# The order of P5 and P6 by halves of d_ff, and of one layer-2 unit, in a sparse attention and MLP kernel

## The chip, the cores and the metric

One core of one Trainium2 chip. The core has five engines with an instruction queue each, which run beside each other and wait for each other by semaphores: TensorE (PE in the profile; its weight loads are shown as PEld), VectorE (DVE), ScalarE (ACT), GpSimd (POOL) and SyncE (SP, which here only issues DMAs). The metric is the device time of the whole kernel in microseconds (us). Before the change it is 301.54 us, the median of three runs (301.05 to 302.14).

## The reference

Sparse attention over 8 batches, 8 heads, 576 positions and head size 64, in two patterns, and then a two-layer MLP with a leaky activation over the 4608 tokens:

```python
rel = pos[:, None] - pos[None, :]
mask_local = (rel >= 0) & (rel < stride)                  # stride 32; heads 0 to 3
mask_strided = (rel >= 0) & (pos[None, :] % stride == pos[:, None] % stride)   # heads 4 to 7
scores = np.where(masks[None], scale * np.matmul(q, k.transpose(0, 1, 3, 2)), -1000000000.0)
attn = np.exp(scores - scores.max(-1, keepdims=True))
attn_out = np.matmul(attn / (attn.sum(-1, keepdims=True) + 1e-09), v)
x = attn_out.transpose(0, 2, 1, 3).reshape(4608, 512)
h = x @ w_in                                              # w_in 512 x 2048
g = np.maximum(h, 0.0) + alpha * np.minimum(h, 0.0)
out = g @ w_out                                           # w_out 2048 x 512
```

## The kernel before

Everything that is multiplied is float16, sums are float32 in PSUM. The tokens are worked through in nine chunks of 512 (`n` = 0 to 8). A chunk has a layer 1 and a layer 2; between these matmuls stand the pieces of the attention whose output the next chunks need. One program order is written out by hand: each helper records its instructions with `keep`, and on every engine they stand in the order in which they were recorded.

Layer 1 (`lin1_piece`, L573): for each of the 16 blocks of d_ff, four matmuls into a PSUM tile `hps`, a negative part on ScalarE (`neg`, L593) and a combination on VectorE into `gT` (L596, recorded one step later).

Layer 2 of chunks 2 to 8 (`lin2_fast`, L673) uses seven products of half size in place of eight, P1 to P7, on sums of blocks. Each of them has, for each of two blocks of 128 tokens (`r`; in the products by sums a token half `z`), eight matmuls of 128x256 over the eight pairs of d_ff blocks (`y`). The sums of `wout` are made once (`wsum`, four tiles), those of `gT` once a chunk (`gsum`, four tiles, L643 and L654): each is made in two halves, `h` = 0 for y 0 to 3 and `h` = 1 for y 4 to 7, on VectorE or GpSimd. The table `sums` says behind which of the chunk's 30 steps; steps 0 to 15 are layer 1, 16 and 17 are P1, 18 and 19 P5, 20 and 21 P6, then P2, P7, P3, P4 (P4 and P3 are interleaved in the last chunk):

```python
sums = {
    5: [(2, 0, "pool")], 9: [(0, 0, "pool")], 15: [(0, 1, "dve"), (1, 0, "dve")],
    16: [(1, 1, "dve")], 18: [(2, 1, "dve")], 19: [(3, 0, "dve")], 20: [(3, 1, "dve")]}
```

P5 is gsum0 by wsum0, P6 is gsum1 by wsum1. In chunks 2 to 7 P5 already takes its halves of d_ff one after the other, for both token halves each (`both`, matmuls at L709); P6 takes one token half with all eight `y`, and then the other (L719). In the last chunk P5 does so too, and its second token half goes to a PSUM tile of its own, `bank["f"]`. P1 goes to bank a and is copied to bank b (L733), on which P6 and then P7 and P4 add; P5 stands in bank e. ScalarE copies P5 and P6 to `par` tiles in SBUF (L736, in the last chunk L727 for each half of P5), which VectorE adds to later results on their way out (`store`, L656, L665).

Attention pieces run between these steps (`attn_step`, L557): scores of a pair of heads (`score_both`, L333, matmuls at L353, into one `sp` tile of two banks and two `sph` tiles), the exp on ScalarE (L376, L382), the mask on GpSimd (L378, L385), the product with v (`pv_piece`, L390, matmuls L406), and its scaling on VectorE (reciprocal L413, multiply L415, into `x16` or `x16s`). `pv`, `sph`, transposed tiles `tp` and `xp` all come from one pool of three PSUM buffers (`pspool`), used in turn: each waits until the engine that reads the buffer's last content has read it.

Layer 2 of chunk 0 is spread by hand over the attention of batch 1 (list at L901). `U(kf)` is a unit of three 128x512 matmuls (L875) for one block of d_ff, into three PSUM tiles that no attention piece uses; `W(i)` does the chunk's last 128 tokens. `T(2, "q")` and `T(2, "k")` turn the local heads' q and k (`transpose_piece`, L254, nine transposes at L269 into two `tp` tiles, copied to SBUF by ScalarE, L207, and VectorE, L209). `Pv(g, i)` is the i-th product with v of pair g. The stretch that the change touches runs `Pv(7, 1), U(6), T(2, "q"), Pv(7, 2), U(7), T(2, "k"), Pv(6, 1), U(8)`.

Of the kernel before, what the change touches and what calls it, by code (L numbers as in the profile page):

```python
# [9 lines left out]
F32 = mybir.dt.float32  # L10
# [22 lines left out]
def kernel(  # L33
# [10 lines left out]
    nc = tc.nc  # L44
    keep = tc.keep_in_program_order
# [15 lines left out]
    npool = ctx.enter_context(tc.tile_pool(name="np", bufs=2))  # L61
    opool = ctx.enter_context(tc.tile_pool(name="op", bufs=4))
    pspool = ctx.enter_context(tc.tile_pool(name="ps", bufs=3, space=bass.MemoryType.PSUM))
# [8 lines left out]
    wsum = [cpool.tile([128, 8, 256], F16, name=f"wsum{i}") for i in range(4)]  # L72
    gsum = [cpool.tile([128, 8, 256], F16, name=f"gsum{i}") for i in range(4)]
# [180 lines left out]
    def transpose_piece(u, nm):  # L254

        b = u // 2  # L260
        early = b < NEARLY
        src = cast16[(b, False, nm)]
        dst = qTs[u % 2][:, :, 0:576] if nm == "q" else kTs[u % 2][:, :, 32:608]
        o = dst.rearrange("r e (p t) -> r e p t", t=9)
        tps = []
        for t0, t1 in ((0, 5), (5, 9)):
            tp = pspool.tile([128, 8, 64, 2], F16, tag="ps", name="tp")
            for t in range(t0, t1):
                keep(nc.tensor.transpose(  # L269
                    tp[:, t - t0].rearrange("r p e -> r (p e)"), src[:, t].rearrange("p f d -> p (f d)"), ident))  # L270
            tps.append(tp[:, 0 : t1 - t0].rearrange("r t p e -> r e p t"))
        cast_copy("act", o[:, :, :, 0:5], tps[0])
        cast_copy("dve" if early and (u or nm == "k") else "act", o[:, :, :, 5:9], tps[1])
# [116 lines left out]
    def pv_piece(P, a):  # L390
        while defer and any(P.et[z][0] is defer_et["et"] for z in P.et):
            defer.pop(0)()
        if P.x16 is None:
            if P.xd and P.strided:
                P.x16 = x16s
            else:
                P.x16 = xpool.tile([128, 1024], F16, tag="x16", name="x16")
        v16 = cast16[(P.b, P.strided, "v")]
        grp = P.pgroups[a]
        r = 72 if P.strided else 128  # L400
        pv = pspool.tile([128, 512], F32, tag="ps", name="pv")
        nb = 2 * len(grp)
        for x in range(nb):
            t, hh = grp[x // 2], x % 2
            et, c = P.et[(t, hh)]
            keep(nc.tensor.matmul(  # L406
                pv[:, 65 * x : 65 * x + 65], et[0:r, c : c + 128],
                v16[0:r, 2 * P.pr + hh, t, :] if P.strided else v16[:, 6 * (2 * P.pr + hh) + t, :],
                start=(x == 0), stop=(x == nb - 1), skip_group_check=True))
        w = P.w  # L410
        rc = rpool.tile([128, 8], F32, tag="rc", name="rc")
        pvv = pv[0:w, 0 : 65 * nb].rearrange("r (c e) -> r c e", e=65)
        keep(nc.vector.reciprocal(rc[0:w, 0:nb], pvv[:, :, 64]))  # L413
        c0 = 128 * grp[0]
        keep(nc.vector.tensor_tensor(  # L415
            P.x16[0:w, c0 : c0 + 64 * nb].rearrange("r (c e) -> r c e", e=64),
            pvv[:, :, 0:64],
            rc[0:w, 0:nb].unsqueeze(2).to_broadcast([w, nb, 64]), op=ALU.mult))
# [46 lines left out]
    def T(u, nm):  # L465
        return lambda: transpose_piece(u, nm)
# [4 lines left out]
    def Pv(g, i):  # L471
        return lambda: pv_piece(pairs[g], i)
# [198 lines left out]
    bank = {}  # L671

    def lin2_fast(n, i):  # L673

        last = n == NCH - 1
        x, r = (("1", i) if i < 2 else ("5", i - 2) if i < 4 else ("6", i - 4) if i < 6 else ("2", i - 6) if i < 8
                else ("7", i - 8) if i < 10 else ("3", i - 10) if i < 12 else ("4", i - 12))  # L680
        if last and i > 10:
            x, r = (("4", 0), ("4", 1), ("3", 1))[i - 11]
        b = {"1": "a", "2": "a", "5": "e", "3": "e"}.get(x, "b")
        first = x in "15" and r == 0
        if first:
            bank[b] = phpool.tile([128, 512], F32, tag="hps", name="ops")
        o = bank[b][:, 256 * r : 256 * r + 256]
        if last and b == "e" and r == 1:
            if x == "5":
                bank["f"] = pspool.tile([128, 512], F32, tag="ps", name="opsl")  # L690
                first = True
            o = bank["f"][:, 0:256]

        def g(t, j):
            return lambda y: gTs[n][:, 2 * y + j, 256 * t + 128 * r : 256 * t + 128 * r + 128]

        def s(z):
            return lambda y: gsum[z][:, y, 128 * r : 128 * r + 128]

        def w(j, c):  # L700
            return lambda y: wout16[:, 2 * y + j, 256 * c : 256 * c + 256]

        def t(z):
            return lambda y: wsum[z][:, y, :]

        def both(h):
            for z in range(2):
                for y in range(4 * h, 4 * h + 4):
                    keep(nc.tensor.matmul(  # L709
                        bank["e"][:, 256 * z : 256 * z + 256], gsum[0][:, y, 128 * z : 128 * z + 128], wsum[0][:, y, :],  # L710
                        start=(z == 0 and y == 0), stop=(y == 7), skip_group_check=True))

        lhs, rhs = {
            "1": (g(0, 0), w(0, 0)), "2": (g(0, 1), w(1, 0)), "3": (s(3), w(1, 1)),
            "4": (g(1, 1), t(3)), "5": (s(0), t(0)), "6": (s(1), t(1)), "7": (s(2), t(2))}[x]
        if x == "5" and not last:
            both(r)
        for y in range(8 if x != "5" or last else 0):
            keep(nc.tensor.matmul(  # L719
                o, lhs(y), rhs(y), start=(first and y == 0), stop=(y == 7), skip_group_check=True))  # L720
        if last and x == "3":
            store(n, 0, 1, bank["f" if r else "e"], bank["s6"], r)
            return
        if last and x == "5":
            if r == 0:
                bank["s5"] = npool.tile([128, 512], F32, tag="par", bufs=2, name="par")
            keep(nc.scalar.copy(bank["s5"][:, 256 * r : 256 * r + 256], o))  # L727
            return
        if r == 0:
            return  # L730
        if x == "1":
            bank["b"] = phpool.tile([128, 512], F32, tag="hps", name="ops")
            keep(nc.scalar.copy(bank["b"], bank["a"]))  # L733
        elif x in "56":
            z = npool.tile([128, 512], F32, tag="par", bufs=2, name="par")
            keep(nc.scalar.copy(z, bank[b]))  # L736
            bank["s" + x] = z
        elif x == "2":
            store(n, 0, 0, bank["a"])
        elif x == "7":  # L740
            late.append(lambda: store(n, 1, 1, bank["b"], bank["s5"]))
        elif x == "3":
            late.append(lambda: store(n, 0, 1, bank["e"], bank["s6"]))
        else:
            store(n, 1, 0, bank["b"])
# [12 lines left out]
    def warm(n):  # L758

        for _ in range(n):  # L760
# [12 lines left out]
            name=nc.get_next_instruction_name(), act_func_set_id=6, ins=[], outs=[]  # L773
# [96 lines left out]
    def U(kf):  # L870
        def run():
            if kf == 0:
                banks.extend(phpool.tile([128, 512], F32, tag="hps", name="ops") for _ in range(3))
            for mt in range(3):
                keep(nc.tensor.matmul(  # L875
                    banks[mt], gTs[0][:, kf, 128 * mt : 128 * mt + 128], wout16[:, kf, :],
                    start=(kf == 0), stop=(kf == 15)))
            if kf == 15:
                for mt in range(3):
                    osb = opool.tile([128, 512], F32, tag="osb", name="osb")  # L880
                    cast_copy("dve" if mt == 1 else "act", osb, banks[mt])
                    keep(nc.sync.dma_start(out[128 * mt : 128 * mt + 128, :], osb))
        return run
# [16 lines left out]

    for fn in [  # L901
        U(0), Cl(1, "q"), G("k", 1), vs(1, 0), vs(1, 1), sc1(6), U(1), U(2), sc1(7), Cl(1, "k", "act"), U(3), U(4), loads2,
        Pv(6, 0), Pv(7, 0), Pv(6, 2), U(5), Pv(7, 1), U(6), T(2, "q"), Pv(7, 2), U(7), T(2, "k"), Pv(6, 1), U(8),
        X(7, "dve"), W(0), W(1), sc1(4), U(9), W(2), sc1(5), W(3), ov(1, "dve", 0, 24), W(4), U(10), X(6), U(11),
        Pv(4, 1), W(5), Pv(4, 0), Cl(2, "q", "act"), U(12), Cl(2, "k", "act"), Pv(5, 1), U(13), U(14), Pv(5, 0), U(15), W(6), X(5), X(4), W(7)]:
        fn()
# [65 lines left out]
```

## Time and profile before

| what | value |
|---|---|
| median of three runs | 301.54 us |
| the profiled execution's own time | 301.32 us |
| its span, first to last instruction | 299.5 us |
| granted TensorE clock, mean | 1.000 of full speed |
| attention of batch 1 with chunk 0's layer 2 | about 38 to 58 us |
| chunk 1; 2; 3 | 58 to 92; 92 to 124; 124 to 154 us |
| chunk 4; 5; 6 | 154 to 185; 185 to 215; 215 to 244 us |
| chunk 7; 8 | 244 to 270; 270 to 299.5 us |

The profile is of one execution. Its page gives busy times and the chain of work that ended last; the trace behind it answers with lists of waits and with timelines, whose times count from the span's start. A row of a timeline merges instructions of the same kind that follow each other on an engine: start, length from the first start to the last end, engine, line, what, how many; in brackets how long the engine was idle before and what ended that. `out<-in` names the tiles. Matmuls overlap each other, so a row's length is more than the number of matmuls by their spacing.

### The profile page before, as it was taken

The numbers are of one execution on the slowest core, as the hardware profiler recorded it, in microseconds if no ns is written. First come the engines' busy times: TensorE is split into PE (matmuls) and PEld (weight loads), VectorE is DVE, ScalarE is ACT, GpSimd is POOL, SyncE is SP. The second block draws the span as 40 slices with busy tenths as digits, with TensorE's granted clock in tenths as the row PEclk, the third lists the DMA queues.
The fourth block names the chain that finished last, engine by engine and source line by source line (L and its number), as shares of the span: only waits on it lengthen the run. The fifth ranks groups of instructions, "written<-read, shape, count | busy, mean of one in ns | idle before, by whom it ended". The sixth has DMA issues, their size and how long they took to land.

```text
span 299.5 us, 6826 instructions
## 1 busy us (share of the span) xinstructions
PE 293.3 (98%) x2683; PEld 182.7 (61%) x2683; DVE 219.0 (73%) x408; ACT 179.1 (60%) x332; POOL 171.9 (57%) x160
## 2 busy tenths in 40 slices
PE   8999999999999999999999999999999999999995
PEld 3764545554555477646874687468745974784584
DVE  5677886668775897589848984898489958926852
ACT  1676764698457775776467646764676356516730
POOL 8462271049959998979897988494653405002200
PEclk9999999999999999999999999999999999999999
DMA  7999999999998969999989999965811040022004
GB/s 187 256 195 197 244 194 257 218 176 315 117 201 150 113 101 81 161 194 142 124 149 182 137 150 178 195 95 89 206 23 21 18 146 0 2 72 70 0 2 141
DMA packets 96976, 41.18 MB, mean 138 GB/s; under 512 B 75360, under 2 KB 93232, under 8 KB 96944
## 3 DMA queue, kind: packets, MB, share of 16 engines
q0 software_dynamic: 51008, 17.77, 60.1%
q1 hardware_dynamic: 45584, 22.32, 35.7%
q10 hardware_dynamic: 352, 0.66, 0.8%
q8 instruction: 21, 0.34, 0.5%
q14 instruction: 11, 0.09, 0.1%
HBM read 38.24 MB, written 9.44 MB: 159 GB/s over the span
## 4 chain that ended last, share of the span: by engine, by line
PE 85%; DVE 7%; ACT 3%; issue 3%; DVEq 0%; ACTq 0%
PE hps L585 37%; PE ops L719 22%; PE ops L624 5%; PE pv L406 4%; PE ops L875 3%; PE wps L761 3%; DVE gsum L654 2%; DVE gT L596 2%; PE sp L353 2%; ACT neg L593 1%; PE xp L431 1%; PE sph L353 1%; PE ops L890 1%; PE ops L709 1%; ACT et L382 1%
## 5 line engine op out<-in xcount | busy, mean ns | idle before, releaser
L585 PE MATMUL hps<-xT,win 128*128 128x512 f16 x576 | 131.9, 379 | 0.0
L596 DVE SCALAR_TENSOR_TENSOR gT<-neg,oma,hps 128x512 f16<-128x512 f32 x144 | 105.2, 744 | 36.1 <-ACT neg L593 28.2
L593 ACT ACTIVATE neg<-hps 128x512 f32<-128x512 f32 x144 | 85.9, 598 | 35.1 <-PE hps L585 32.9
L585 PEld LDWEIGHTS <-win 128*128 128x128 f16 x576 | 53.7, 98 | 58.8 <-issue 0.2
L654 POOL TENSOR_TENSOR gsum<-gT 128x1024 f16<-128x1024 f16 x14 | 29.7, 2125 | 41.7 <-DVE gT L596 36.7
L378 POOL TENSOR_TENSOR et<-et,consts 128x576 f16<-128x576 f16 (+1 forms) x24 | 34.7, 1447 | 29.8 <-ACT et L376 29.6
L719 PEld LDWEIGHTS <-gsum 128*128 128x128 f16 x352 | 32.2, 98 | 5.8 <-DVE gsum L654 1.8
L719 PEld LDWEIGHTS <-gT 128*128 128x128 f16 x336 | 31.5, 98 | 5.4 <-issue 0.3
L415 DVE TENSOR_TENSOR x<-pv,rc 96x384 f16<-96x384 f32 (+2 forms) x62 | 33.0, 532 | 2.1
L385 POOL TENSOR_TENSOR et<-et,consts 128x576 f16<-128x576 f16 (+1 forms) x24 | 31.5, 1312 | 0.0
L719 PE MATMUL ops<-wsum,gsum 128*128 128x256 f16 x232 | 30.2, 273 | 0.3
L406 PEld LDWEIGHTS <-et 72*128 72x128 f16 (+1 forms) x448 | 23.4, 98 | 11.3 <-issue 1.4
L719 PE MATMUL ops<-wout,gT 128*128 128x256 f16 x224 | 27.9, 272 | 0.1
L376 ACT ACTIVATE et<-sp 128x576 f16<-128x576 f32 (+1 forms) x24 | 15.5, 645 | 17.8 <-PE sp L353 17.8
L413 DVE RECIPROCAL rc<-pv 96x6 f32<-96x6 f32 (+2 forms) x80 | 14.6, 183 | 10.7 <-PE pv L406 10.4
L211 POOL COPY vs<-stv 72x1024 f16<-72x1024 f16 x12 | 13.3, 1116 | 15.6 <-DMA stv<-in_v_dram 15.6
L665 DVE TENSOR_TENSOR osb<-ops,par 128x512 f32<-128x512 f32 (+1 forms) x14 | 9.4, 673 | 15.9 <-PE ops L719 8.2
L382 ACT ACTIVATE et<-sph 128x288 f16<-128x288 f32 (+1 forms) x48 | 18.8, 409 | 0.0
L663 ACT COPY osb<-ops 128x512 f32<-128x512 f32 x14 | 8.2, 588 | 16.7 <-PE ops L719 16.6
L624 PE MATMUL ops<-wout,gT 128*128 128x512 f16 x64 | 16.4, 379 | 0.0
L406 PE MATMUL pv<-vs,et 72*128 72x65 f16 x256 | 15.4, 193 | 0.9 <-ACT qT L207 0.5
L736 ACT COPY par<-ops 128x512 f32<-128x512 f32 x13 | 7.6, 587 | 13.3 <-PE ops L709 7.5
(107 smaller groups left out, 353.3 us busy)
## 6 DMA issues: line engine op xcount, KB each, us to landing
out_dram<-osb SPq DMA_DIRECT2D x35, 256.0 KB, 4.0
vl<-in_v_dram POOLq DMA_DIRECT2D x6, 384.0 KB, 9.2
win<-in_moe_w_in_dram POOLq DMA_DIRECT2D x4, 512.0 KB, 16.9
wout<-in_moe_w_out_dram POOLq DMA_DIRECT2D x4, 512.0 KB, 17.4
qsd<-in_q_dram POOLq DMA_DIRECT2D x7, 288.0 KB, 6.6
ksd<-in_k_dram POOLq DMA_DIRECT2D x7, 288.0 KB, 7.9
stv<-in_v_dram POOLq DMA_DIRECT2D x7, 288.0 KB, 8.2
ql<-in_q_dram SPq DMA_DIRECT2D x3, 576.0 KB, 7.1
```

The source lines that it names most:

```text
L376: keep(nc.scalar.activation(ev.rearrange("r (y c) -> r y c", y=2), sp[0:r, :, 0:n], AF.Exp, scale=SCALE))
L378: keep(nc.gpsimd.tensor_tensor(mv, mv, m, op=ALU.mult))
L382: keep(nc.scalar.activation(ev[:, n * y : n * y + n], sps[y][0:r, 0:n], AF.Exp, scale=SCALE))
L385: keep(nc.gpsimd.tensor_tensor(mv, mv, m, op=ALU.mult))
L406: keep(nc.tensor.matmul(pv[:, 65 * x : 65 * x + 65], et[0:r, c : c + 128], v16[0:r, 2 * P.pr + hh, t, :] if P.strided else v16[:, 6 * (2 * ...
L415: keep(nc.vector.tensor_tensor(P.x16[0:w, c0 : c0 + 64 * nb].rearrange("r (c e) -> r c e", e=64), pvv[:, :, 0:64], rc[0:w, 0:nb].unsqueeze ...
L585: keep(nc.tensor.matmul(hps, win16[:, kk, 128 * m : 128 * m + 128], xT[:, kk, c0 : c0 + 512], start=(kk == 2), stop=(kk == 1)))
L593: keep(nc.scalar.activation(neg, hps, AF.Relu, scale=-1.0))
L596: keep(nc.vector.scalar_tensor_tensor(gTs[n][:, m, :], neg, oma[:, m : m + 1], hps, op0=ALU.mult, op1=ALU.add))
L624: keep(nc.tensor.matmul(ops, gTs[n][:, kf, 128 * mt : 128 * mt + 128], wout16[:, kf, :], start=(kf == 0), stop=(kf == 15)))
L654: keep((nc.vector if eng == "dve" else nc.gpsimd).tensor_tensor(gsum[i][:, hs], a, b, op=op))
L719: keep(nc.tensor.matmul(o, lhs(y), rhs(y), start=(first and y == 0), stop=(y == 7), skip_group_check=True))
```

## The change

P6 takes the halves of d_ff one after the other for both token halves in all of chunks 2 to 8, and P5 does so in the last chunk too; `both` now serves both products, opens bank f at its first call in the last chunk, and the two copies of P5 into its `par` tile stand behind the second half there. In the list of batch 1, `U(7)` and `Pv(7, 2)` change places. The number and the kind of instructions stay the same on every engine.

```diff
         if last and b == "e" and r == 1:
-            if x == "5":
-                bank["f"] = pspool.tile([128, 512], F32, tag="ps", name="opsl")
-                first = True
             o = bank["f"][:, 0:256]
...
         def both(h):
+            if x == "5" and h == 0 and last:
+                bank["f"] = pspool.tile([128, 512], F32, tag="ps", name="opsl")
             for z in range(2):
+                i, alone = int(x) - 5, x == "5" and last and z == 1
+                o = bank["f"][:, 0:256] if alone else bank[b][:, 256 * z : 256 * z + 256]
                 for y in range(4 * h, 4 * h + 4):
                     keep(nc.tensor.matmul(
-                        bank["e"][:, 256 * z : 256 * z + 256], gsum[0][:, y, 128 * z : 128 * z + 128], wsum[0][:, y, :],
-                        start=(z == 0 and y == 0), stop=(y == 7), skip_group_check=True))
+                        o, gsum[i][:, y, 128 * z : 128 * z + 128], wsum[i][:, y, :],
+                        start=(x == "5" and y == 0 and (z == 0 or alone)), stop=(y == 7), skip_group_check=True))
...
-        if x == "5" and not last:
+        if x in "56":
             both(r)
-        for y in range(8 if x != "5" or last else 0):
+        for y in range(0 if x in "56" else 8):
             keep(nc.tensor.matmul(
                 o, lhs(y), rhs(y), start=(first and y == 0), stop=(y == 7), skip_group_check=True))
...
-        if last and x == "5":
-            if r == 0:
-                bank["s5"] = npool.tile([128, 512], F32, tag="par", bufs=2, name="par")
-            keep(nc.scalar.copy(bank["s5"][:, 256 * r : 256 * r + 256], o))
+        if last and x == "5" and r:
+            bank["s5"] = npool.tile([128, 512], F32, tag="par", bufs=2, name="par")
+            for z, o in enumerate((bank["e"], bank["f"])):
+                keep(nc.scalar.copy(bank["s5"][:, 256 * z : 256 * z + 256], o[:, 0:256]))
             return
...
-        Pv(6, 0), Pv(7, 0), Pv(6, 2), U(5), Pv(7, 1), U(6), T(2, "q"), Pv(7, 2), U(7), T(2, "k"), Pv(6, 1), U(8),
+        Pv(6, 0), Pv(7, 0), Pv(6, 2), U(5), Pv(7, 1), U(6), T(2, "q"), U(7), Pv(7, 2), T(2, "k"), Pv(6, 1), U(8),
```

## The prediction

> **What bounds the kernel now.** I read the page first (busy shares, then the chain that ended last), then the list of waits, then the timeline around each place that the diff touches.
>
> ```profile
> span 299.5 us, 6826 instructions
> ...
> PE 293.3 (98%) x2683; PEld 182.7 (61%) x2683; DVE 219.0 (73%) x408; ACT 179.1 (60%) x332; POOL 171.9 (57%) x160
> ...
> PE 85%; DVE 7%; ACT 3%; issue 3%; DVEq 0%; ACTq 0%
> ```
>
> TensorE sets the time: busy 98% of the span and 85% of the chain, at a granted clock of 1.00 all through. The change adds and removes no instruction on any engine; on TensorE some matmuls stand elsewhere, and the orders of VectorE, ScalarE, GpSimd and SyncE, with their DMAs, are as before. So nothing is moved past a DMA queue, and all that can change is how long TensorE stands in waits. These are the two kinds of wait that the moved instructions bear on (engine and line, releaser, us in total, times, longest):
>
> ```profile
> PEld L719 <- DVE gsum L654: 1.8, 6, 0.4
> ...
> PE pv L406 <- ACT qT L207: 0.5, 1, 0.5
> ```
>
> So at most some 2.3 us of 299.5 is on offer. The 1.8 is more than TensorE loses: a weight load is idle a while before any matmul too. The matmuls tell the loss. In the P products they start 0.109 us apart (the chain has 16 of L719 in 1.75 us where none waits); what a gap has beyond that is lost.
>
> **P6 in chunks 2 to 5.** Before, the four second-half matmuls of token half 0 are the 5th to 8th of P6; after, the second halves are the 9th to 16th, so a late second half of gsum1 gets 4 x 0.109 = 0.44 us more. Chunk 3 (start, us, engine, line, what; idle before in brackets):
>
> ```profile
> 143.03 0.68 DVE L654 TENSOR_TENSOR gsum<-gsum,gT 128x1024 f16<-128x1024 f16 x1
> 143.04 0.35 PEld L719 LDWEIGHTS <-gsum 128*128 128x128 f16 x4
> ...
> 143.76 0.33 PEld L719 LDWEIGHTS <-gsum 128*128 128x128 f16 x4 [0.37 <-DVE gsum L654]
> 143.85 0.55 DVE L415 TENSOR_TENSOR x16s<-pv,rc 72x384 f16<-72x384 f32 x1
> 144.30 0.30 PEld L353 LDWEIGHTS <-kT 64*128 64x128 f16 x12 [0.21 <-issue]
> ...
> 144.44 0.31 PE L353 MATMUL sph<-qT,kT 64*128 64x96 f16 x6
> ```
>
> The four loaded first start from 143.07, so the fourth at 143.40, and the fifth at 143.76: 0.36 - 0.109 = 0.26 us lost, until 0.05 after gsum ended (143.03 + 0.68 = 143.71). The change takes that away. But what is late next? Behind these eight matmuls TensorE has the scores of the next pair: six into `sp`, then six into two `sph` tiles. The second `sph` tile takes the PSUM buffer of the second pv tile, so its weight load waits for VectorE's x16s that reads it: 143.85 + 0.55 = 144.40, and 0.05 later is 144.45. The first `sph` matmul stands at 144.44, so the second is already there on the stroke of that release. VectorE is busy without a gap from 140.7 to 147.4 and gains nothing from TensorE being early. So the 0.26 us moves from L719 to L353 and the gain is 0; by what the score would do if it did not wait, it is 0.26. Chunks 4 and 5 repeat the pattern (174.07 and 204.41, idle 0.36 and 0.37; x16s ends 174.71 and 205.05; `sph` starts 174.76 and 205.10). In chunk 2 the loss is 113.18 - 112.92 - 0.109 = 0.15 (first matmul at 112.58), but what follows the eight is a pv whose load already stands idle 0.36 until 113.88 for x16s of 113.27 + 0.55 = 113.82: gain 0. In chunks 6 and 7 no L719 load waits for gsum there: 0. Taken: 0; bounds 0 and 0.15 + 3 x 0.26 = 0.93 us.
>
> A side effect: in chunks 3 to 5 the `sp` scores, their exp on ScalarE and so GpSimd's mask (L378, 145.44) come 0.26 sooner, before VectorE's gsum3 (two at 145.47) instead of with it. The masks alone take 1.28 (L378 at 138.73); this one took 2.44 beside the two gsums, so one of the two is held. If now VectorE is held, by a mask's 1.28, what is late? Its next results have 1.45 us to spare at L719's P4 (it needs the store of 149.93 + 0.69 = 150.63 and starts at 152.08), and VectorE itself idles 0.57 + 0.22 + 0.29 before that store: 2.5 us of cover in all. Priced at 0.
>
> The Trainium skill ("SBUF — State Buffer", Who interferes with whom) says that a VectorE instruction with two SBUF inputs and a GpSimd one that reads SBUF shut each other out, and that the one that issued first keeps the port to its end. By that rule the mask would win here and VectorE lose up to 1.28 us a chunk, against nothing if it still loses as at 145.44; the sum stays the same by both, and the case where the rule costs is the last rival.
>
> **P5 of the last chunk.** The same order, on the last chunk's bank e and its spare bank f:
>
> ```profile
> 285.24 0.69 DVE L654 TENSOR_TENSOR gsum<-gT 128x1024 f16<-128x1024 f16 x1
> ...
> 285.98 2.95 PEld L719 LDWEIGHTS <-gsum 128*128 128x128 f16 x28 [0.29 <-DVE gsum L654]
> ```
>
> The first matmul starts at 285.37, so the fourth at 285.70, and the fifth at 285.98: 0.29 - 0.109 = 0.18 lost. After, the second half is needed at 285.37 + 8 x 0.109 = 286.24, past 285.93 + 0.05: no wait. No attention is left to hold what follows; TensorE then runs in one piece to 296.3, and gsum1's halves (done 286.53 and 287.13, needed 287.12 and 287.99) are in time. So 0.18 us comes off the end. P6 there loses nothing before (eight at a time from 287.31), so its own new order is worth 0. The two copies into `par` (0.37 each, L727) now both come after the second half; their reader, the store of P7, starts at 292.80, five us later, so they cost 0 (0.37 if that cover were gone).
>
> **The unit behind q's turning.** In batch 1, after T(2, "q"), TensorE now does U(7) first and then Pv(7, 2).
>
> ```profile
> 43.40 0.79 PE L269 MATMUL tp<-consts,ql 128*128 128x128 f16 x9
> ...
> 43.88 0.76 ACT L207 COPY qT<-tp 128x640 f16<-128x640 f16 x1 [1.29 <-PE tp L269]
> ...
> 44.34 0.71 DVE L209 COPY qT<-tp 128x512 f16<-128x512 f16 x1
> 44.69 0.28 PE L406 MATMUL pv<-vs,et 72*128 72x65 f16 x4 [0.50 <-ACT qT L207]
> ...
> 44.80 0.81 PE L875 MATMUL ops<-wout,gT 128*128 128x512 f16 x3
> ...
> 45.96 0.35 PE L406 MATMUL pv<-vs,et 72*128 72x65 f16 x6
> ...
> 48.15 0.39 PE L353 MATMUL sph<-qT,kT 64*128 64x96 f16 x6
> ```
>
> The pv takes the PSUM tile that ScalarE empties until 43.88 + 0.76 = 44.64, so it can't start before 44.69, and TensorE could go on from 44.02 (the ninth transpose starts at 43.97, and they are 0.055 apart). The unit's three matmuls take 45.46 - 44.80 = 0.65 (to the start of the next transpose) and wait for nothing: in the new place 44.02 to 44.68. They fill the hole and the pv starts at 44.69 as before. Its four take 0.12, so k's transposes start at 44.80 instead of 45.46. They are held once: the second tile's buffer is the one VectorE empties until 44.34 + 0.71 = 45.05, so its four start at 45.10 and end at 45.32. Behind them stands Pv(6, 1), whose buffer is that of the moved pv; VectorE reads it with a reciprocal at 45.01 and a multiply at 45.22 for 0.42, to 45.64, and these do not move, since the pv didn't. So Pv(6, 1) starts at 45.69 instead of 45.96: 0.26 kept of the 0.65, the other 0.39 a new wait on VectorE. Further on the six `sph` of sc1(4) took 0.39 where others take 0.31: they were held 0.08 by xT's copy (47.46 + 0.74 = 48.20). VectorE's k copy (after 45.64 instead of at 46.16) and with it that copy are 0.5 earlier, TensorE 0.26, so this goes too, 0.09 by the starts. Together 0.35 us. All later work of the batch waits for TensorE or for what it feeds, so it keeps it. Bounds: 0.65 if the reader's wait fell away, 0 if the hole opens again later.
>
> **The sum.** 0.35 + 0.18 + 0 = 0.53 us: span 299.5 to 299.0. The profiled execution took 301.32, 1.82 outside the span, so 300.8; it lies 0.2 under the median of the three runs shown (301.54; 301.05 to 302.14), from which it would be 301.0.
>
> **Rivals.**
> 1. P6's gain lands in chunks 2 to 5 as well. For it: the six waits are there and go. Against: the x16s rows, within 0.01 us of where `sph` starts. It gives 0.53 + 0.93 = 1.46, 299.9.
> 2. Batch 1's 0.35 is swallowed. For it: GpSimd's cast of the next strided v (L211) waits 15.6 us for its load, until 61.5, and that load doesn't come sooner. Against: no wait of TensorE for GpSimd is in the list. It gives 0.18: 301.1.
> 3. Slower: the earlier masks take the port from VectorE in chunks 3 to 5. With mask, v cast and mask in front (1.28 + 1.03 + 1.26 = 3.57, the rows at 145.44, 147.84 and 148.84) VectorE could be up to 3.6 late; from 2.5 it decides, at P4's store. At 3.1 it costs 3 x 0.6 - 0.53 = +1.3: 302.6. Against: GpSimd's queue would have to win three times in a row.
> 4. The order does not take effect: 301.3. Against it: the waits on gsum1's second half do stand at the ninth matmul in the built kernel.
>
> **How the numbers follow.** The forecast 0.55, the first rival 0.15, the second 0.12, the third 0.08, the fourth 0.01, and 0.09 for what I don't see, on both sides alike. 0.3% is 0.9 us, about what a measurement of this kernel can tell from no change, and the forecast is 0.17%: runs of one kernel lie 1.1 us apart, so 0.20 of its 0.55 may well be measured as faster. Faster: 0.15 + 0.20 + 0.05 = 0.40; slower: 0.08 + 0.04 = 0.12; the rest 0.48. The likeliest is 300.8. The range goes from the first rival (299.9, and 0.1 for scatter) to 302.0, past the second and the scatter of the runs; the third lies outside.
>
> **What would show it.** Right: in batch 1 the wait of pv for ScalarE's qT is gone and a pv waits some 0.4 us for VectorE's x around 45.7; from 58 to 284 us everything stands 0.35 earlier; in chunks 3 to 5 no L719 load waits for gsum, and a L353 load waits 0.26 for x16s; layer 1 of chunk 4 starts no more than 0.4 earlier than at 154.25; the last chunk's P5 has no wait. Wrong: chunks 3 to 5 each shorter by 0.2 or more, or gsum3 rows of over 0.7 us with TensorE late behind them.

## The result and the profile after

The changed kernel takes 300.69 us (median of 12 runs, 300.37 to 301.06) against 301.22 for the kernel before (12 runs, 301.05 to 302.14): a ratio of 0.9981 with a 95% interval of 0.9972 to 0.9990. That is 0.53 us less (0.3 to 0.8 by the interval). The prediction took 0.3% as about what a measurement can tell from no change; with twelve runs on each side this 0.2% can be told. The profiled execution of it took 300.67 us. The new code shifts line numbers by one: the matmuls of P1 to P7 that stood at L719 are at L720, those of `both` at L710, the `par` copies at L737 and L728, the units' matmuls at L876.

The page of the changed kernel, in its first lines and in the chain that ended last:

```profile
span 298.9 us, 6826 instructions
...
PE 292.9 (98%) x2683; PEld 183.0 (61%) x2683; DVE 219.1 (73%) x408; ACT 178.8 (60%) x332; POOL 172.8 (58%) x160
...
PE 82%; DVE 10%; ACT 3%; issue 3%; DVEq 0%; ACTq 0%
```

The span is 0.6 shorter. VectorE works as long as before (219.1 against 219.0 us), yet its share of the chain has risen from 7% to 10%: the chain now passes through VectorE at places where it passed through TensorE. The list of waits of the changed kernel (engine and line, releaser, us in total, times, longest) says where:

```profile
PEld L353 <- DVE x16s L415: 0.6, 3, 0.2
...
PEld L406 <- DVE x16s L415: 0.5, 1, 0.5
PE pv L406 <- DVE x L415: 0.5, 2, 0.2
```

The row of 1.8 us for loads of gsum and the row of 0.5 us for a pv behind ScalarE's qT are gone, and these stand in their place. First the timeline of the changed kernel in batch 1, around `U(7)`:

```profile
43.94 0.81 PE L876 MATMUL ops<-wout,gT 128*128 128x512 f16 x3
...
44.61 0.28 PE L406 MATMUL pv<-vs,et 72*128 72x65 f16 x4
...
44.73 0.68 PE L269 MATMUL tp<-consts,kl 128*128 128x128 f16 x9
45.14 0.42 DVE L415 TENSOR_TENSOR x<-pv,rc 72x256 f16<-72x256 f32 x1
...
45.62 0.24 PEld L406 LDWEIGHTS <-et 72*128 72x128 f16 x6 [0.39 <-DVE x L415]
45.62 0.36 PE L406 MATMUL pv<-vs,et 72*128 72x65 f16 x6 [0.22 <-DVE x L415]
...
47.82 0.29 PE L353 MATMUL sph<-qT,kT 64*128 64x96 f16 x6
```

The unit fills the hole ahead of the pv, which starts at 44.61. k's transposes follow at 44.73 in place of 45.46, but `Pv(6, 1)` has to wait for VectorE's x (45.14 + 0.42 = 45.56) until 45.62, where it stood at 45.96. The `sph` scores' 0.39 us of before is 0.29. (0.09 us of each of these starts is no gain: at 42 us, ahead of all that was changed, this execution already stood 0.09 earlier than the one before.)

Then chunk 3 of the changed kernel, at the place of the wait that the new order of P6 was to remove:

```profile
142.62 1.04 PE L710 MATMUL ops<-wsum,gsum 128*128 128x256 f16 x8
...
143.39 0.55 DVE L415 TENSOR_TENSOR x16s<-pv,rc 72x384 f16<-72x384 f32 x1
...
143.59 0.20 PEld L353 LDWEIGHTS <-kT 64*128 64x128 f16 x7 [0.21 <-issue]
...
143.73 0.57 PE L353 MATMUL sph<-qT,kT 64*128 64x96 f16 x6
...
144.00 0.15 PEld L353 LDWEIGHTS <-kT 64*128 64x128 f16 x5 [0.21 <-DVE x16s L415]
...
144.72 2.70 POOL L378 TENSOR_TENSOR et<-et,consts 128x576 f16<-128x576 f16 x1 [1.02 <-ACT et L376]
145.01 1.28 DVE L654 TENSOR_TENSOR gsum<-gT,gsum 128x1024 f16<-128x1024 f16 x2
```

P6's eight run without a gap. The six `sph` then take 0.57 in place of 0.31 us, because the load at 144.00 waits for the x16s that ends at 143.39 + 0.55 = 143.94: the stall is the same 0.26 us (0.57 - 0.31; the load itself is shown idle for 0.21), now at the eighth of the twelve score loads (seven go from 143.59 on). The two gsum3 at 145.01 take 1.28, as long as two took at 145.47 in the kernel before, though the record has a mask begin 0.29 us ahead of them; it is the mask that is stretched, to 2.70. In the last chunk of the changed kernel P5 and P6 load without a wait:

```profile
284.80 3.48 PEld L710 LDWEIGHTS <-gsum 128*128 128x128 f16 x32
```

Where the time came from can be read by taking the start of each TensorE instruction in a kernel's trace less the start of the same instruction before. The change of that difference over a stretch is what the stretch gained (minus) or lost:

| kernel | median, us | ratio (95%) | batch 1 | chunk 2 | chunk 3 | chunk 4 | chunk 5 | last P5 |
|---|---|---|---|---|---|---|---|---|
| changed kernel | 300.69 | 0.9981 (0.9972 to 0.9990) | -0.34 | 0.00 | -0.01 | +0.01 | -0.01 | -0.19 |
| swap of U(7) alone | 300.69 | 0.9982 (0.9971 to 0.9994) | -0.33 | -0.03 | -0.02 | -0.01 | -0.02 | 0.00 |
| P6 alone | 301.27 | 1.0006 (0.9996 to 1.0015) | 0.00 | -0.05 | -0.03 | 0.00 | -0.02 | -0.01 |
| last P5 alone | 300.91 | 0.9989 (0.9981 to 0.9998) | 0.00 | -0.03 | -0.03 | 0.00 | -0.02 | -0.19 |
| gsum1's half later | 300.37 | 0.9976 (0.9965 to 0.9986) | -0.34 | -0.15 | -0.03 | -0.01 | -0.02 | -0.19 |
| x16s first | 299.46 | 0.9945 (0.9932 to 0.9957) | -0.33 | -0.13 | -0.37 | -0.34 | -0.35 | -0.19 |
| x16s first, P6 and P2 in turns | 299.15 | 0.9931 (0.9919 to 0.9944) | -0.34 | -0.42 | -0.40 | -0.39 | -0.41 | -0.19 |
| x16s first, old P6 | 302.86 | 1.0056 (1.0042 to 1.0070) | -0.35 | +0.39 | +0.54 | +0.55 | +0.54 | -0.19 |
| U(8) forward too | 300.48 | 0.9980 (0.9971 to 0.9989) | -0.41 | -0.04 | -0.03 | 0.00 | -0.02 | -0.19 |

Chunks 6 and 7 and the rest of chunk 8 are within 0.02 in all of them. For the changed kernel the stretches add up to 0.54, the difference of the medians is 0.53. The kernel before took 301.25 us (31 runs) beside the first four experiments and 301.14 (15 runs) beside the other four.

### The profile page after: what moved, and what is told of

The parts are those of the page before. It is cut to its first block, busy times and chain, and to the rows that moved or that the text cites. A ratio compares the mean times of both kernels' runs of the same rounds, so it can differ in the third digit from the quotient of the medians.

```text
span 298.9 us, 6826 instructions
## 1 busy us (share of the span) xinstructions
PE 292.9 (98%) x2683; PEld 183.0 (61%) x2683; DVE 219.1 (73%) x408; ACT 178.8 (60%) x332; POOL 172.8 (58%) x160
## 4 chain that ended last, share of the span: by engine, by line
PE 82%; DVE 10%; ACT 3%; issue 3%; DVEq 0%; ACTq 0%
PE hps L585 37%; PE ops L720 18%; PE ops L624 5%; PE ops L710 4%; PE pv L406 4%; DVE gsum L654 2%; PE wps L762 2%; PE ops L876 2%; DVE gT L596 2%; DVE x L415 2%; PE sp L353 2%; DVE x16s L415 1%; ACT neg L593 1%; PE sph L353 1%; PE xp L431 1%
## 5 line engine op out<-in xcount | busy, mean ns | idle before, releaser
L378 POOL TENSOR_TENSOR et<-et,consts 128x576 f16<-128x576 f16 (+1 forms) x24 | 35.5, 1481 | 30.2 <-ACT et L376 30.0
L720 PEld LDWEIGHTS <-gT 128*128 128x128 f16 x336 | 31.5, 98 | 5.4 <-issue 0.3
L385 POOL TENSOR_TENSOR et<-et,consts 128x576 f16<-128x576 f16 (+1 forms) x24 | 31.5, 1313 | 0.0
L720 PE MATMUL ops<-wout,gT 128*128 128x256 f16 x224 | 27.9, 272 | 0.1
L710 PE MATMUL ops<-wsum,gsum 128*128 128x256 f16 x216 | 26.6, 273 | 0.0
L720 PEld LDWEIGHTS <-gsum 128*128 128x128 f16 x224 | 20.9, 98 | 2.6
L710 PEld LDWEIGHTS <-gsum 128*128 128x128 f16 x224 | 20.8, 98 | 2.6
```

The source lines that it names most:

```text
L378: keep(nc.gpsimd.tensor_tensor(mv, mv, m, op=ALU.mult))
L385: keep(nc.gpsimd.tensor_tensor(mv, mv, m, op=ALU.mult))
L710: keep(nc.tensor.matmul(o, gsum[i][:, y, 128 * z : 128 * z + 128], wsum[i][:, y, :], start=(x == "5" and y == 0 and (z == 0 or alone)), st ...
L720: keep(nc.tensor.matmul(o, lhs(y), rhs(y), start=(first and y == 0), stop=(y == 7), skip_group_check=True))
```

## The experiments: one part at a time

Each of the first three makes one part of the change alone. The swap of `U(7)` and `Pv(7, 2)` alone:

```diff
-        ... T(2, "q"), Pv(7, 2), U(7), T(2, "k"), Pv(6, 1), U(8),
+        ... T(2, "q"), U(7), Pv(7, 2), T(2, "k"), Pv(6, 1), U(8),
```

> The kernel before with only U(7) and Pv(7, 2) changed places. My theory: this part alone is worth 0.35 us (0.26 at Pv(6, 1), 0.09 at the sph scores), all of it kept to the end: 301.22 - 0.35 = 300.87, and from 58 us on every engine stands 0.35 earlier. Rival (its gain is swallowed by the load that GpSimd waits for at 61.5 us): 301.2, and the shift is gone by 110 us.

Measured: 300.69 us; 0.33 us gained in batch 1, and kept to the end. The median is that of the whole change, and its interval (0.18 to 0.87 us less) is too wide to tell this part from the whole; the trace tells them apart.

The new order of P6 alone, in chunks 2 to 8 (the loop inside `both`, not shown, serves P6 as well, as in the change):

```diff
-        if x == "5" and not last:
+        halves = x == "6" or x == "5" and not last
+        if halves:
             both(r)
-        for y in range(8 if x != "5" or last else 0):
+        for y in range(0 if halves else 8):
```

> The kernel before with only P6 by halves, in all chunks from 2; P5 of the last chunk as before. My theory: worth nothing, 301.22 within 0.05: the L719-line waits for gsum in chunks 3 to 5 go, and the loads of the scores wait as long for x16s. Rival (the gain lands): 0.93 us, 300.3. The other rival (masks earlier, VectorE held): gsum3 rows of over 0.7 us after the scores of chunks 3 to 5, time above 301.5.

Measured: 301.27 us, ratio 1.0006, no difference; over chunks 2 to 5 the trace shows 0.10 us, in steps of at most 0.05. In its chunk 3 the wait is where it is in the changed kernel:

```profile
144.02 0.55 PE L353 MATMUL sph<-qT,kT 64*128 64x96 f16 x6
...
144.27 0.15 PEld L353 LDWEIGHTS <-kT 64*128 64x128 f16 x5 [0.19 <-DVE x16s L415]
```

So the rival by which P6's 0.93 us lands as well falls. The one by which the earlier masks hold VectorE falls by the trace: the two gsum3 take 1.28 us here as well (at 145.28), and the mask beside them is the one that is stretched. The time alone, whose interval reaches 0.15% above no change, would not have excluded its 301.5.

The new order of P5 in the last chunk alone:

```diff
-        if x == "5" and not last:
+        if x == "5":
             both(r)
```

(with `bank["f"]` opened in `both` and the two copies behind the second half, as in the change).

> The kernel before with only the last chunk's P5 by halves. My theory: 0.18 us, 301.04; up to 285 us nothing moves, from 286 us all is 0.18 earlier. Rival (the ScalarE copies of P5, now both behind the second half, hold the end): 301.2 or more, with the store of P7 waiting for a copy.

Measured: 300.91 us (0.06 to 0.57 less by the interval); by the trace nothing that this part could have made until 285 us, then 0.19 at once, and no more behind it. The swap's 0.33 and this 0.19 make 0.52 of the 0.54 us of the whole. Drifts of 0.08 to 0.10 us over chunks 2 to 5 stand in all three traces, whichever part was made, so they are not the new order's; what they come from is open.

## The experiments: what holds chunks 3 to 5

That P6 gained nothing was laid to the x16s behind which the scores wait. Is VectorE as such too late there, or does only its order stand in the way? With the new order of P6, gsum1's second half is needed later than before: by the 0.44 us of the four matmuls that now stand ahead of it, which the prediction counted, and by the twelve scores too, which stand between the two halves and which it did not count. (In the run below the halves start at 142.35 and 143.71, 1.36 us apart; before, the fifth matmul was due 0.44 us after the first. So the slack is 0.92 us.) But the table of sums still puts that half ahead of the x16s. The changed kernel with that half one step later:

```diff
-        16: [(1, 1, "dve")], 18: [(2, 1, "dve")], 19: [(3, 0, "dve")], 20: [(3, 1, "dve")]}
+        17: [(1, 1, "dve")], 18: [(2, 1, "dve")], 19: [(3, 0, "dve")], 20: [(3, 1, "dve")]}
```

> The changed kernel with the second half of gsum1 made one step later on VectorE, behind the x16s that the scores of chunks 3 to 5 wait for. If only that x16s stands in the way (a free PSUM buffer is all the scores lack), it is done 0.6 us sooner, the second half of gsum1 is not needed until after the scores, and each of chunks 3 to 5 gains its 0.26 us, chunk 2 some 0.4: 300.69 - 1.1 = 299.6. If VectorE as such is behind (it works from 140.7 to 147.4 without a gap, and the same sum of work has to be done before P6 can go on), the wait goes back to the gsum1 loads and chunks 3 to 5 gain 0 to 0.05 each, with at most chunk 2's 0.4 left: 300.3 to 300.7. I hold the second.

Measured: 300.37 us, 0.15 us gained in chunk 2 and 0.01 to 0.03 in chunks 3 to 5. The timeline of its chunk 3:

```profile
142.35 1.04 PE L710 MATMUL ops<-wsum,gsum 128*128 128x256 f16 x8
...
142.98 0.68 DVE L654 TENSOR_TENSOR gsum<-gsum,gT 128x1024 f16<-128x1024 f16 x1
...
143.46 0.29 PE L353 MATMUL sph<-qT,kT 64*128 64x96 f16 x6
143.57 0.68 DVE L654 TENSOR_TENSOR gsum<-gT 128x1024 f16<-128x1024 f16 x1
...
143.71 1.05 PE L710 MATMUL ops<-wsum,gsum 128*128 128x256 f16 x8
...
144.38 0.42 DVE L415 TENSOR_TENSOR x16s<-pv,rc 72x256 f16<-72x256 f32 x1
...
144.95 0.34 PE L406 MATMUL pv<-vs,et 72*128 72x65 f16 x6 [0.19 <-DVE x16s L415]
```

The scores don't wait any more (0.29), and gsum1's second half is in time (142.98 + 0.68 = 143.66). But the pv behind P6 stands at 144.95, where the eight matmuls would let it go at 143.71 + 8 x 0.109 = 144.58: 0.37 us lost to the third x16s (144.38 + 0.42 = 144.80, and its release). In the kernel before that pv already lost 0.13 (144.69 + 0.87 = 145.56, started 145.69). The stall has moved once more, now the whole of 0.26 us onto a loss of 0.13. So the time is the one of the theory that was held, but not for its reason: no gsum1 load waits in chunks 3 to 5, and it was a second x16s that held TensorE there. And again a sum stands ahead of that x16s, the half of gsum2 at 143.57, which P7 needs only later. So one more entry of the table was moved:

```diff
-        17: [(1, 1, "dve")], 18: [(2, 1, "dve")], 19: [(3, 0, "dve")], 20: [(3, 1, "dve")]}
+        17: [(1, 1, "dve")], 19: [(2, 1, "dve"), (3, 0, "dve")], 20: [(3, 1, "dve")]}
```

> The changed kernel with two of VectorE's sums later: gsum1's second half behind step 17 (as in the run before) and gsum2's second half behind step 19 instead of 18, so that in chunks 3 to 5 each x16s multiply stands on VectorE ahead of the sum half that is needed later than it. Theory (TensorE's loss in chunks 3 to 5 is a matter of the order on VectorE; the halves order of P6 gave slack that the old sums table didn't use): the wait of the second sph load (0.26 us a chunk) and the 0.19 to 0.26 us wait of the pv on the third x16s both go, some 0.4 us a chunk for three chunks, beside 0.13 in chunk 2: 300.69 - 1.2 = 299.5 us (299.2 to 299.8), and no L353 or L406 load waits for x16s in chunks 3 to 5. Rival (VectorE as such is behind, whatever its order): the wait moves on to the loads that need gsum2 or gsum3, 300.3 to 300.5 us, as with gsum1's half alone.

Measured: 299.46 us, as the theory had it; VectorE as such is not behind there, only its order was in the way. Its chunk 3:

```profile
143.93 0.29 PE L353 MATMUL sph<-qT,kT 64*128 64x96 f16 x6
...
144.19 1.05 PE L710 MATMUL ops<-wsum,gsum 128*128 128x256 f16 x8
...
144.26 0.42 DVE L415 TENSOR_TENSOR x16s<-pv,rc 72x256 f16<-72x256 f32 x1
144.60 0.68 DVE L654 TENSOR_TENSOR gsum<-gT 128x1024 f16<-128x1024 f16 x1
...
145.07 0.35 PE L406 MATMUL pv<-vs,et 72*128 72x65 f16 x6
```

The pv starts at 145.07, when 144.19 + 0.87 = 145.06 lets it: scores and pv both without a wait. The 0.26 that had been pushed along and the 0.13 of the pv are both gone, 0.39 less 0.01 by these rows; chunks 3 to 5 measured 0.37, 0.34 and 0.35. No load in its list of waits is held by x16s. What is left is in chunk 2, two P6 loads:

```profile
112.46 0.77 PEld L710 LDWEIGHTS <-gsum 128*128 128x128 f16 x8 [0.16 <-DVE gsum L654]
...
113.75 0.77 PEld L710 LDWEIGHTS <-gsum 128*128 128x128 f16 x8 [0.24 <-DVE gsum L654]
```

The next run puts a token half of P2, which needs no gsum, between the halves of P6. What was expected of it was written before these two rows were known:

```diff
-        x, r = (("1", i) if i < 2 else ("5", i - 2) if i < 4 else ("6", i - 4) if i < 6 else ("2", i - 6) if i < 8
+        x, r = (("1", i) if i < 2 else ("5", i - 2) if i < 4 else (("6", 0), ("2", 0), ("6", 1), ("2", 1))[i - 4] if i < 8
```

> The run before, and P6 and P2 in turns: first half of P6, token half 0 of P2, second half of P6, token half 1 of P2, so that gsum1's second half is needed 0.87 us later still. Theory (in the run before no matmul waits for gsum1 any more): no difference, within 0.1 us of it (299.4 to 299.6). Rival (gsum1's second half is still the last wait there): up to 3 x 0.2 = 0.6 us less, 298.9 us.

Measured: 299.15 us. The intervals of the two ratios overlap, but the traces tell them apart: chunk 2 gains another 0.29, where the wait of 0.24 at the second half is gone; chunks 3 to 5 gain 0.03 to 0.06 each, and what these come from is open. So the expectation of no difference missed chunk 2, and the rival was right there and not in chunks 3 to 5. It is the fastest version of this study, 0.9931 of the kernel before (0.9919 to 0.9944).

Last, the same order on VectorE, but P6 token half by token half as in the kernel before:

```diff
-        if x in "56":
+        if x == "5":
             both(r)
-        for y in range(0 if x in "56" else 8):
+        for y in range(0 if x == "5" else 8):
```

> VectorE's order of the run before the last, and the rest of the change, but P6 token half by token half as in the kernel before. Theory (the new order of P6 is worth nothing by itself but is what lets VectorE's order be changed): the fifth matmul of P6 now waits for a half that comes one x16s (0.56 us) later, 0.26 + 0.56 = some 0.8 us a chunk lost where the kernel before lost 0.26; chunks 3 to 5 cost 3 x 0.55 = 1.6 us more than in the changed kernel, some 302.2 us (301.6 to 302.6). Rival (the order of P6 doesn't matter and only VectorE's does): as e5, some 299.5 us.

Measured: 302.86 us, slower than the kernel before (ratio 1.0056, 1.0042 to 1.0070). Its chunk 3:

```profile
143.13 0.60 PE L720 MATMUL ops<-wsum,gsum 128*128 128x256 f16 x4
...
143.76 0.68 DVE L654 TENSOR_TENSOR gsum<-gsum,gT 128x1024 f16<-128x1024 f16 x1
...
144.50 0.61 PE L720 MATMUL ops<-wsum,gsum 128*128 128x256 f16 x4 [0.76 <-DVE gsum L654]
```

The fifth matmul starts at 144.50, where 143.13 + 4 x 0.109 = 143.57 would let it: 0.93 us lost in place of 0.26, 0.67 more. Of this 0.11 comes back at the pv, which now loses 0.02 in place of 0.13 (145.40 + 0.87 = 146.27, started 146.29). That makes 0.56 a chunk, measured 0.54 to 0.55. The expectation had this term right and left out chunk 2, which lost 0.39 too. So 302.86 lies above the range it gave; 0.39 of the 0.66 us between 302.86 and 302.2 is chunk 2, and the rest is no more than the five runs scatter (302.54 to 303.10). The same two entries of the table are thus worth 1.2 us with the new order of P6 (300.69 to 299.46) and cost 2.2 us with the old one (302.86 against the same 300.69, in which the order of P6 by itself is worth nothing; 2.0 by the stretches of the table above). The new order of P6 gains nothing by itself, and is what makes that gain possible.

## The experiment in batch 1

Of the 0.65 us that `U(7)` takes, 0.39 became a wait of `Pv(6, 1)` for VectorE's x. Another unit fits into that hole:

```diff
-        ... U(7), Pv(7, 2), T(2, "k"), Pv(6, 1), U(8),
+        ... U(7), Pv(7, 2), T(2, "k"), U(8), Pv(6, 1),
```

> The changed kernel with U(8) also ahead of Pv(6, 1), into the new hole of batch 1 where Pv(6, 1) waits some 0.39 us for VectorE's x. Theory (behind that hole TensorE meets work that VectorE or ScalarE sets, as when 0.26 of the 0.65 us came out of the first swap): Pv(6, 1) and what VectorE does behind it come later, 0.0 to 0.1 us gained, 300.6 to 300.7 us. Rival (TensorE alone sets the end there): the whole 0.39 us is kept, 300.3 us.

Measured: 300.48 us; batch 1 gains 0.41 in place of 0.34 us. The hole is filled, and the next one opens behind it, in the scores of sc1(4):

```profile
46.97 0.74 DVE L209 COPY xT<-xp 128x576 f16<-128x576 f16 x1
...
47.43 0.62 PE L353 MATMUL sph<-qT,kT 64*128 64x96 f16 x6
47.77 0.14 PEld L353 LDWEIGHTS <-kT 64*128 64x128 f16 x4 [0.28 <-issue]
```

The six `sph` take 0.62 in place of 0.29: they go on at 47.77, 0.06 after VectorE's copy of xT ended (46.97 + 0.74 = 47.71). The row names no releaser ("issue"); that it is this copy is read from the times alone. So 0.33 of the 0.39 is lost again 2 us further on, and the theory stands by the trace, which gives 0.07 us, though the median lies 0.1 below the 300.6 to 300.7 that it named. The medians alone, 300.48 and 300.69, are too close to tell it from its rival.

## Why the prediction was right, step by step

- **The bound.** TensorE sets the end, and what can change is how long it stands in waits: shown by the traces. What each part saved on TensorE by itself is still there at the end of its trace. The medians of the single parts (0.56, -0.02 and 0.34 us less) agree with that within their intervals, but are too coarse to show it.
- **P6 in chunks 2 to 5, 0.** Right, in size and in place. In chunk 2 the pv's load, idle 0.36 before, is idle 0.53 us in the changed kernel; in chunks 3 to 5 the second `sph` load waits for x16s. What the step called "VectorE is busy without a gap ... and gains nothing from TensorE being early" was true of the order that the table gave VectorE and was not a limit of VectorE: with the same work in another order TensorE gains 0.34 to 0.37 us a chunk. The prediction didn't ask what the slack could be used for, and counted it too small: 0.44 us, without the scores between the two halves, where the rows of the run with gsum1's half later give 0.92. No term of the sum rests on that.
- **The side effect on the masks, 0.** Right: the gsum3 rows stay at 1.28 for two, and TensorE loses nothing behind them. What was left open was which of the two is held; it is the mask. Of the forecasts by the Trainium skill's rule ("SBUF — State Buffer", Who interferes with whom), the one in which the earlier mask wins did not come: 144.72 to 147.42 for a mask that takes 1.27 alone, beside two undisturbed sums that began 0.29 after it. That one of the two stands until the other is through does show: the mask ends 1.13 us after the sums do, where alone it takes 1.27. No run here shows why the mask is the one that stands, and the profile's spans on GpSimd are rough, their starts included. (The prediction's "last rival" for this case is its third.)
- **P5 of the last chunk, 0.18.** Measured 0.19, all of it at the place named.
- **Batch 1, 0.35.** Measured 0.34: pv no longer waits for qT, `Pv(6, 1)` waits with its load idle for 0.39 us as named, and the `sph` row fell from 0.39 to 0.29.
- **The sum, 0.53.** Measured 0.53 (301.22 to 300.69); that it agrees to the last digit is luck, with an interval of 0.3 to 0.8. The firmer figure is the 0.54 of the trace, place by place. The likeliest time was 300.8, made from a profiled execution of 301.32, which lay 0.1 above the median of more runs.
- **The rivals.** P6's gain landing as well: fell with P6 alone (301.27). Batch 1's gain swallowed: fell with the swap alone, whose 0.33 us is still there at the end. Masks that hold VectorE: the sums were not held in the changed kernel, nor with P6 alone. The order not taking effect: the waits moved as the new order has it.
- **A sign that was drawn too sharply.** Layer 1 of chunk 4 was to start at most 0.4 us earlier, and starts 0.46 earlier. 0.09 of it was there at 42 us, ahead of all that the change touches, so 0.37 is the change's. A bound on a start has to leave room for how the beginnings of two executions differ.

## What to carry to other kernels

Here a stall that an in-order engine no longer had at one place went to the next instruction whose release didn't come sooner: in whole in chunks 3 to 5, by 0.39 of 0.65 us in batch 1. Before pricing a stall's removal, walk on through the queue to the next buffer or operand that the other engine sets, and compare that release with the new arrival; here one such step ate 0.26 us in each of three chunks, and a second stood behind it. When a reordering turns a tight need into slack, look at once at what stands ahead of the newly late thing on the releasing engine, and give that slack away: in this kernel the two belonged together, and either without the other was worth nothing or less.

## What was not expected of the hardware

- Beginnings differ. At 42 us, ahead of all changed work, TensorE stood between 0.39 earlier and 0.21 later than in the trace of before, in kernels that are alike up to there. One profile's span can thus be off by as much as the swap is worth; differences within a trace are far steadier (batch 1's gain was 0.33 to 0.35 in the six traces that have the swap and nothing else new in that batch).
- A load of TensorE that the traces show waiting for VectorE starts 0.05 to 0.06 us after the recorded end of what it waits for (x16s 143.94, load 144.00; x 45.56, load 45.62), at every such place from 12 us on in all ten traces, which is why gains of 0.1 us could be predicted at all. Where the trace has a pv's matmul wait and not its load, it can be 0.15 us (144.80 to 144.95 in the run with gsum1's half later).
- GpSimd's mask and VectorE's sums hold each other up, in both directions: at 140.69 in the kernel before a gsum half took 1.12 us instead of 0.68, and ended 0.56 after a mask that ran from 139.97 for its 1.28; at 144.72 in the changed kernel the mask took 2.70 and the sums nothing extra. Wherever sums stretch a mask in chunks 3 to 5, in all ten traces, it ends 1.13 to 1.14 us after the last of them, whether its record begins 0.29 ahead of the first (the changed kernel) or 0.66 behind it (the old P6 with x16s first). Undisturbed, the same masks take 1.27 to 1.30. So it had done some 0.15 us at most when the sums were through, and the recorded start of a mask doesn't tell which of the two goes first. What decides between them was not tried.
